# Reordering casts, transposes, loads and one layer's start around a TensorE-bound attention and mixing kernel

## The chip, the cores and the metric

The kernel runs on one core of one Trainium2 chip. The metric is the device time of one execution in microseconds (us). TensorE is the matmul engine (PE in the profile, PEld its weight loads), VectorE is DVE, ScalarE is ACT, GpSimd is POOL, and SP is the sync engine, which here only issues transfers. "Position" below is the start of an instruction in us from the start of the span. PSUM is the memory that the matmuls write into and that the other engines copy results out of.

## The reference, cut to what matters

There are 8 batches. Each goes through cross attention between x (8 heads, 512 rows, 64 wide) and a state of 32 rows, then a two-dimensional Fourier mix, a normalization and a two-layer network (512 to 2048 to 512).

```python
scores  = scale * x @ state.T ;  xread = softmax(scores) @ state      # per head
scores2 = scale * state @ x.T ;  sread = softmax(scores2) @ x
x  = concat([xread, sread]) reshaped to (8, 544, 512)
u  = x + real(fft(fft(x, axis=1), axis=2))
un = (u - mean(u)) / sqrt(var(u) + 1e-6)
out = u + relu(un @ w_ch1) @ w_ch2
```

## The kernel before

Everything is bf16 on TensorE with f32 in PSUM. The program fixes the order of instructions on each engine. From batch 1 on, each period `weave`s several streams by their place between 0 and 1: layer 2 of one batch, layer 1 of the next (`ph`, from `unT`), the reads of attention (`xfp`, `xlp`, `xrp`), the Fourier transform (`gp`, `yp`, then `U`, statistics, `ub`, and its turned form `unT`), the scores (`esp`) of a later one, and loads of x. More names that recur: `warm` are matmuls on the identity whose results nothing uses; `sT` and `xT` are the state and x turned, `eTp` holds scores made from them (or their turned form), `srp` the reads on the state's side; `XF`, `XR`, `XL` are the reads as VectorE copies them out of PSUM, and the fold is the chain, mostly on VectorE, from these to `XQ`, which `gp` needs; `tp` is the turn of `ub` on TensorE; `po` is layer 2's output and `ot` a result tile.

```python
    def cast_x(b):                       # x to bf16
        if b == 0:
            for si in (0, 1, 3):
                nc.scalar.copy(t[:, si, 1:513], xs[:, si, :])
            nc.gpsimd.tensor_copy(t[:, 2, 1:513], xs[:, 2, :])
    ...
    def clears(i):                       # GpSimd, set 0: after it has issued four weight loads
        nc.gpsimd.memset(XFs[i][:, :, 512:514], 0.0)
        nc.gpsimd.memset(XRs[i][:, :, 0:514:513], 0.0)
        ...
        def turn_u(k, r):                # batches 0 and 1: on TensorE, copied out of PSUM
            ...
            if b >= u_by_dma:            # batches 2 and up: by a transposing transfer
                nc.sync.dma_start_transpose(out=unT[:, :, col:col + 128], in_=ub[k, r])
                return
    ...
    for b in range(1, B + 1):
        streams = [(l2_now + ..., 0, 1)]
        if b < B:
            streams.append((layer1(b), 0.08, 1))
        if b + 1 < B:
            streams.append((reads_next, 0, 0.34))
            streams.append((transform(b + 1), 0.47 if b == 1 else 0.4, 0.77 if b == 3 else 0.8))
        ...
        weave(*streams)
```

The softmax here doesn't subtract the row's maximum and nothing guards it: scores larger than these inputs give would overflow.

## Time and profile before

| | before |
|---|---|
| time, median of 4 runs | 315.04 us (314.83 to 316.01) |
| span of the profiled execution | 313.9 us |
| TensorE / VectorE / ScalarE / GpSimd busy | 95% / 59% / 44% / 24% |
| idle TensorE before the first matmul | 3.4 us |
| listed TensorE waits that the change aims at | 3.5 us |

How to read it: the profile's list of waits gives, for each line of TensorE, what ended the idle time before it, the sum, the number and the longest. In a timeline, a row is a start, a duration, the engine, line, operation and tiles, and in brackets the idle time before it with its releaser. The rows themselves are in the prediction.

### The profile page before, as it was taken

Reading aid. Unit: us, or ns where it says so; the run is one execution under the profiler, and the core shown is the slowest. Engines: PE = TensorE matmul, PEld = TensorE weight load, DVE = VectorE, ACT = ScalarE, POOL = GpSimd, SP = SyncE. Lnnn points to the kernel's source line nnn. Section 1 sums busy time; section 2 is a strip of 40 time slices with the busy share of each in tenths; the row PEclk is TensorE's granted clock in tenths of the full one; section 3 lists DMA queues with packets and bytes.
Section 4 is the critical chain, followed back from the end, with each engine's and each line's share of the span. In section 5 each row is a group of like instructions: output and inputs, shape, how many; then the busy total and the mean of one; then the engine's idle time right before and its main releaser. Section 6 shows DMA issues by size and latency. Waiting matters only on the chain.

```text
span 313.9 us, 5948 instructions
## 1 busy us (share of the span) xinstructions
PE 299.2 (95%) x2300; PEld 170.2 (54%) x2300; DVE 185.0 (59%) x442; ACT 137.6 (44%) x268; POOL 75.0 (24%) x171
## 2 busy tenths in 40 slices
PE   5778999999989999999999999999999999999995
PEld 5566997544544555456644554455445544555443
DVE  8696882877767593873817774686559563100012
ACT  6698764735533543243442444333533433333300
POOL 8758784410240040300510024002200131000000
PEclk9999999999999999999999999999999999999999
DMA  9999899965654925349344343631333036303147
GB/s 161 183 200 203 140 177 167 198 123 138 112 101 104 185 68 136 77 102 157 87 84 98 87 102 76 128 83 51 80 75 67 33 84 98 74 34 67 38 100 165
DMA packets 114292, 34.86 MB, mean 111 GB/s; under 512 B 105688, under 2 KB 110040, under 8 KB 114264
## 3 DMA queue, kind: packets, MB, share of 16 engines
q1 hardware_dynamic: 103544, 28.72, 45.8%
q0 software_dynamic: 4224, 4.19, 8.7%
q10 hardware_dynamic: 6496, 1.57, 2.4%
q8 instruction: 18, 0.29, 0.4%
q14 instruction: 10, 0.08, 0.1%
HBM read 22.41 MB, written 14.02 MB: 116 GB/s over the span
## 4 chain that ended last, share of the span: by engine, by line
PE 76%; DVE 15%; DMA 3%; ACT 3%; issue 1%; SPq 0%; DVEq 0%; ACTq 0%
PE po L763 31%; PE ph L698 27%; PE gp L578 3%; PE ph L708 3%; DVE U L548 3%; DVE st L318 2%; DMA xs<-in_x_dram 2%; DVE ub L612 1%; PE po L755 1%; PE xfp L436 1%; PE yp L544 1%; DVE ot L729 1%; PE xrp L436 1%; PE gp L582 1%; PE yp L543 1%
## 5 line engine op out<-in xcount | busy, mean ns | idle before, releaser
L763 PE MATMUL po<-w,hT 128*128 128x512 bf16 x496 | 125.2, 379 | 0.0
L700 ACT ACTIVATE hT<-ph 128x512 bf16<-128x512 f32 x112 | 66.9, 597 | 125.0 <-PE ph L698 125.0
L698 PE MATMUL ph<-unT,w 128*128 128x512 bf16 x448 | 114.6, 379 | 1.4 <-DMA unT<-ub 1.1
L698 PEld LDWEIGHTS <-w 128*128 128x128 bf16 x576 | 51.1, 98 | 49.9 <-issue 2.3
L763 PEld LDWEIGHTS <-hT 128*128 128x128 bf16 x496 | 47.0, 98 | 44.1
L729 DVE SCALAR_TENSOR_TENSOR ot<-po,rstd,U 128x512 f32<-128x512 f32 (+2 forms) x33 | 24.1, 732 | 52.2 <-PE po L763 47.9
L588 POOL COPY GL<-G 128x128 bf16<-128x128 bf16 x8 | 2.3, 292 | 115.7 <-ACT G L586 115.7
L548 DVE TENSOR_TENSOR U<-yp,XR 128x512 f32<-128x512 f32 x16 | 10.9, 682 | 26.4 <-PE yp L544 26.4
L318 DVE BATCH_NORM_STATS2 st<-U 128x6 f32<-128x512 f32 x32 | 21.8, 682 | 0.1
L324 POOL TENSOR_TENSOR rstd<-mv,epst 128x1 f32<-128x1 f32 x34 | 7.1, 210 | 61.8 <-DVE mv L320 61.8
L325 POOL TENSOR_TENSOR rstd<-rstd,mhalf 128x1 f32<-128x1 f32 x34 | 20.9, 614 | 2.7
L586 ACT CAST G<-gp 128x288 bf16<-128x288 f32 x31 | 12.0, 398 | 11.4 <-PE gp L582 6.8
L708 PE MATMUL ph<-unT,w 128*128 128x128 bf16 x256 | 15.9, 219 | 0.7 <-ACT unT L622 0.7
L783 PE MATMUL warm<-ident 128*128 128x128 bf16 x152 | 12.6, 235 | 3.8 <-POOL ident masks.py:199 3.4
L708 PEld LDWEIGHTS <-w 128*128 128x128 bf16 x256 | 15.0, 98 | 0.9 <-issue 0.8
L578 PEld LDWEIGHTS <-XQ 128*128 128x128 bf16 x96 | 8.9, 98 | 8.8 <-DVE XQ L508 2.3
L783 PEld LDWEIGHTS <-ident 128*128 128x128 bf16 x152 | 10.9, 106 | 4.7 <-POOL ident masks.py:199 3.4
L138 POOL CAST xin<-xs 128x2048 bf16<-128x2048 f32 x7 | 13.2, 1889 | 0.1
L612 DVE TENSOR_SCALAR ub<-U,mv 128x512 bf16<-128x512 f32 x24 | 12.3, 511 | 1.1 <-DVE mv L320 0.3
L436 PEld LDWEIGHTS <-ET 128*128 128x128 bf16 x80 | 7.0, 98 | 9.3 <-DVE XF L445 1.6
L445 DVE TENSOR_TENSOR XR<-xrp,rs 128x512 bf16<-128x512 f32 x16 | 11.1, 695 | 1.1 <-POOL XR L278 0.5
L710 ACT ACTIVATE hT<-ph 128x512 bf16<-128x512 f32 x16 | 9.3, 598 | 3.9 <-PE ph L708 3.9
(190 smaller groups left out, 350.5 us busy)
## 6 DMA issues: line engine op xcount, KB each, us to landing
xs<-in_x_dram SPq DMA_DIRECT2D x22, 256.0 KB, 5.3
w<-in_moe_w_ch_dram POOLq DMA_DIRECT2D x8, 512.0 KB, 10.6
out_dram<-ot SPq DMA_DIRECT2D x15, 256.0 KB, 2.5
r_dram<-ot SPq DMA_DIRECT2D x14, 256.0 KB, 2.3
out_dram<-r_dram SPq DMA_DIRECT2D x14, 256.0 KB, 3.8
xs<-in_x_dram SPq DMA_DIRECT2D x8, 192.0 KB, 4.3
xs<-in_x_dram ACTq DMA_DIRECT2D x2, 256.0 KB, 4.9
l_dram<-ot SPq DMA_DIRECT2D x2, 256.0 KB, 2.0
```

Source lines behind the costliest of these rows:

```text
L318: nc.vector.bn_stats(st6, u)
L325: nc.gpsimd.tensor_tensor(rstd, rstd, mhalf, op=ALU.pow)
L436: nc.tensor.matmul(ph[:, 0:260], lhsT=ET[:, g, c0:c0 + 128], rhs=rhs, start=True, stop=True)
L548: nc.vector.tensor_add(u.rearrange("p (k r) -> p k r", r=2), p.rearrange("p (r k) -> p k r", r=2)[:, 0:u.shape[1] // 2, :], x.rearrange("p ...
L578: nc.tensor.matmul(p[:, 0:NM], lhsT=XQ[:, j, c, :], rhs=tab[c], start=(c == 0), stop=(c == 2 and j != 2))
L612: nc.vector.tensor_scalar(t, in0=ud, scalar1=mv[:, 0:1], scalar2=None, op0=ALU.subtract)
L698: nc.tensor.matmul(ph[:, o:o + n], lhsT=w1[:, c, f * 128:(f + 1) * 128], rhs=un_of[key][:, c, :], start=(c == 0), stop=(c == DC - 1))
L700: nc.scalar.activation(hT[:, per * i:per * i + per, :].rearrange("p a b -> p (a b)"), ph, AF.Relu, scale=-1.0 if key in flipped else 1.0)
L708: nc.tensor.matmul(ph[:, o:o + 128], lhsT=w1[:, c, f * 128:(f + 1) * 128], rhs=un_of[key][:, c, 128 * r:128 * r + 128], start=(c == 0), st ...
L729: nc.vector.scalar_tensor_tensor(ot[:, cols], in0=po_of[i][:, 0:cols.stop - cols.start], scalar=rstd, in1=u[:, cols], op0=ALU.mult, op1=AL ...
L763: nc.tensor.matmul(po_of[i], lhsT=h_of[key][:, f, i * 128:(i + 1) * 128], rhs=w2[:, f, :], start=(f == 0), stop=(f == FC - 1))
L783: nc.tensor.matmul(t[:, 0:128], lhsT=ident, rhs=ident, start=(i == 0), stop=(i == n - 1))
```

## The change

The intent: cast and turn batch 0's pieces in the order in which they land, turn the state before x in the sync queue, load x one period later, start the scores of batch 2 and the first layer of batch 2 later, and let layer 1 of batch 0 begin on half a tile.

```diff
-            for si in (0, 1, 3):
+            for si in (0, 3, 1):                      # casts of batch 0
-            for si in (0, 1, 3, 2):
+            for si in (0, 3, 1, 2):                   # turns of batch 0
-                turned[b] = lambda: (turn_x(0), turn_x(1), turn_state())
+                turned[b] = lambda: (turn_state(), turn_x(0), turn_x(1))
+            if (b, k, r) == (0, 0, 1):                # first copy of unT in two halves
+                for j in (0, 2):
+                    nc.scalar.copy(unT[:, j:j + 2, col:col + 128], tp[...])
+                return
-          ..., (scores_next, 0.4, 1), ([lambda: load_x(4)], 0.6, 0.6))
+          ..., (scores_next, 0.46, 1))
-            streams.append((layer1(b), 0.08, 1))
+            streams.append((layer1(b), 0.13 if b == 2 else 0.08, 1))
-        if b + 4 < B:
-            streams.append(([lambda: load_x(b + 4)], 0.35, 0.35))
+        if b + 3 < B:
+            streams.append(([lambda: load_x(b + 3)], 0.35, 0.35))
```

More of the change, by code (lines that the diff above doesn't have):

```diff
@@ L621, in turn_u @@
                 nc.tensor.transpose(tp[:, 128 * j:128 * j + 128], ub[k, r][:, 128 * j:128 * j + 128], ident)
+            if (b, k, r) == (0, 0, 1):
+                for j in (0, 2):
+                    nc.scalar.copy(unT[:, j:j + 2, col:col + 128],
+                                   tp[:, 128 * j:128 * j + 256].rearrange("p (a b) -> p a b", b=128))
+                return
             (nc.vector.tensor_copy if b == 0 and k else nc.scalar.copy)(unT[:, :, col:col + 128], tp[:, 0:512].rearrange("p (a b) -> p a b", b=128))
@@ L805 @@
     weave((L[11:], 0, 0.25), (t1, 0.2, 1), ([M[i] for i in (0, 4, 1, 5, 2, 6, 3, 7, 8, 9)], 0.33, 0.99),
-          ([lambda: state_blocks(3, B, nc.gpsimd.tensor_copy)], 0.35, 0.35), (scores_next, 0.4, 1), ([lambda: load_x(4)], 0.6, 0.6))
+          ([lambda: state_blocks(3, B, nc.gpsimd.tensor_copy)], 0.35, 0.35), (scores_next, 0.46, 1))
     l2 = M
```

## The prediction

> **What bounds the kernel now.** I read the page's busy row first, then its forty slices, then TensorE's list of waits, and last the timelines around those waits.
>
> ```profile
> PE 299.2 (95%) x2300; PEld 170.2 (54%) x2300; DVE 185.0 (59%) x442; ACT 137.6 (44%) x268; POOL 75.0 (24%) x171
> PE   5778999999989999999999999999999999999995
> ```
>
> TensorE is busy for 299.2 of 313.9 us, so all its idle time is 14.7 us, and the second line shows where it lies: in the first four slices of 7.85 us and in the last one, with one dip in slice 12 (about 86 to 94 us). Outside these the kernel can only get faster by doing less matmul work, and the change removes none. In the chain of waits the two layers' matmuls (po L763 and ph L698) hold 31% and 27% of the span. TensorE's waits, over the whole span:
>
> ```profile
> PE warm L783 <- POOL ident masks.py:199: 3.4, 1, 3.4
> PE xTp L375 <- ACT xin L135: 1.4, 2, 1.1
> PE ph L698 <- DMA unT<-ub: 1.1, 1, 1.1
> PE gp L578 <- DVE XQ L508: 0.8, 2, 0.5
> PE ph L708 <- ACT unT L622: 0.7, 1, 0.7
> PE tp L621 <- ACT ub L610: 0.3, 1, 0.3
> ```
>
> The 3.4 us are the wait for the identity at the start, and some 3.6 us more lie after the last matmul (the last result tile is made by VectorE from 310.31 us, then stored). The change touches neither. What is left is 14.7 - 3.4 - 3.6 = 7.7 us. This is a ceiling, and 2% of the time is 6.3 us. Of it the change aims at four lines: L375 (1.4), the DMA of unT (1.1), L622 (0.7) and L610 (0.3), 3.5 us together.
>
> **What the Trainium skill says.** "Perfetto Trace Analysis", Identifying the Most-Contended Engine, warns that matmul busy time is a poor measure of the distance from the roofline. The trace agrees: one 128x512 matmul is recorded as 379 ns, but groups of four start 0.86 us apart, 0.216 us each. So a small gap in issue can hide under the pipelined ends, and I count gaps by start times. The same page, Optimizing Scalar/DVE Operations, says that breaking up an instruction may let work complete sooner where an engine isn't saturated but leaves bubbles on others, and that ScalarE pays a per-instruction overhead of about 51 ns on PSUM. The trace agrees in size: in the chain a 512-wide copy out of PSUM holds ScalarE for 0.49 us and a 1024-wide one for 0.93, so 0.44 per 512 and 0.05 fixed. "DMA: Bandwidth & Descriptors", Anatomy of one DMA, says that a wait on a semaphore is taken by the issuing sequencer and not by the DMA engines. So one waiting transfer holds back what stands behind it in its queue; below, the sync queue shows just that.
>
> **Part 1: casts of batch 0.** Of the four pieces of x, piece 0 lands at 4.84 us, piece 3 (issued by ScalarE at 1.24, 5.7 us to landing) at about 7.0, and piece 1 (sync queue, 1.74 + 6.84) only at 8.58. Before, ScalarE cast 0, then 1, then 3, and stood from 7.5 to 8.6 with piece 3 already there.
>
> ```profile
> 8.60 1.14 ACT L135 CAST xin<-xs 128x512 bf16<-128x512 f32 x2 [1.08 <-DMA xs<-in_x_dram]
> 8.99 0.68 POOL L136 CAST xin<-xs 128x512 bf16<-128x512 f32 x1 [0.32 <-DMA xs<-in_x_dram]
> 9.64 0.58 ACT L364 COPY sT<-sTp 128x512 bf16<-128x512 bf16 x1
> 10.23 1.01 ACT L376 COPY xT<-xTp 128x1024 bf16<-128x1024 bf16 x1
> ```
>
> In the new order cast 3 fits into that hole, cast 1 runs 8.60 to 9.21, and the copy of sT ends near 9.7 in place of 10.22. Taken alone this is 0.53 us. But the turns also need piece 2, which GpSimd finishes at 8.99 + 0.68 = 9.67, whatever ScalarE does. Then come two transposes (0.28 us), so the copy of xT can start near 10.0 and not at 10.23. Worth 0.22 us. Behind it follows a chain of short steps on VectorE, ScalarE and TensorE up to 28 us. I looked in it for fixed points that would swallow the gain: GpSimd's clears (VectorE waits for one at 14.2), ScalarE's sines (to 23.34, then the G copies), GpSimd's cast of batch 1 (ends 25.72, its turns then start at 25.76 in place of 25.84). Each leaves the long VectorE path just enough room. I carry 0.22 us to 28 us.
>
> **Part 2: first unT copy in two halves.** At 28.22 the chain goes through three copies on ScalarE in a row:
>
> ```profile
> 28.22 0.59 ACT unT L622
> 28.81 0.49 ACT sT L389
> 29.30 0.93 ACT xT L390
> ```
>
> The first half of unT is there about 0.22 us sooner, so the first two matmuls of layer 1 start sooner, but the third needs the second half. More important, TensorE waits again at 30.26, for the third of these copies, and that comes one fixed cost, 0.05 us, later. The 0.67 us wait will look shorter, the time gets 0.05 us worse. Parts 1 and 2 together: 0.17 us.
>
> **Part 3: scores of batch 2 later (0.4 to 0.46).** The order of the built program shows the effect: the first eight score matmuls (0.23 us of issue) move behind the first group of second-axis matmuls yp, and the second eight behind one more layer-2 group. All TensorE work is the same. The first yp starts at 53.20 in place of 53.43, and VectorE's run U, statistics, ub, which begins at 54.14 with an idle VectorE, ends 0.23 us sooner. That run sets the 0.29 us wait at 60.35, which falls to about 0.06. Worth 0.23 us.
>
> **Part 4: state of batch 2 ahead of x, and x one period later.** The sync queue waited 6.8 us for GpSimd's cast before it issued xT, with sT behind it:
>
> ```profile
> 39.21 7.11 SPq L369 DMA_TRANSPOSE xT<-xin  x4
> 46.37 4.19 SPq L358 DMA_TRANSPOSE sT<-stb  x2
> 50.61 10.85 SPq L128 DMA_DIRECT2D xs<-in_x_dram  x12
> 61.56 0.35 SPq L744 DMA_DIRECT2D r_dram<-ot  x1
> ```
>
> The blocks of state are ready at 37.2, so sT uses about 2 us of that wait, and the whole group is issued about 2 us sooner. Yet the first scores at 52.33 show no wait in the trace before, so this buys slack and no time. Of the twelve loads, six (x of batch 4) leave this spot, and the first store of a result, ready at 60.16, no longer stands until 61.56. No matmul waits for it. The loads that now follow at 75 us replace equal loads (batch 5 before); batch 7's come into period 4 near 178, where the sync queue has a hole of 3.8 us for about 4.4 us of issue. Its unT is needed some 10 us later. Worth 0.
>
> **Part 5: layer 1 of batch 2 later (0.08 to 0.13).** This is the largest one.
>
> ```profile
> 90.04 1.04 PE L763 MATMUL po<-w,hT 128*128 128x512 bf16 x4
> 92.14 1.02 PE L698 MATMUL ph<-unT,w 128*128 128x512 bf16 x4 [1.06 <-DMA unT<-ub]
> 93.00 0.38 PE L436 MATMUL xfp<-stb,ET 128*128 128x260 bf16 x2
> 93.22 1.03 PE L763 MATMUL po<-w,hT 128*128 128x512 bf16 x4
> ```
>
> unT of batch 2 lands at 92.0. In the new order the pair xfp (0.22 us) and the next group po (0.86) stand ahead of the first ph: 1.08 us of work that needs no unT, against a wait of 1.06. Its inputs are ready: xfp needs the PSUM tile that VectorE frees at 90.18. The wait goes to about 0, worth 1.06 us. Against this, reads and fold of this period come closer together: I place the last read near 96.9, while VectorE, which first makes a result tile (0.75 us) at 95.2, gets to it at 97.7. From there to the first fold output is 3.1 us as before, at 100.8, while TensorE wants it at 100.6. So I take off 0.2 us for a new wait on XQ.
>
> Sum: 0.17 + 0.23 + 0 + 1.06 - 0.2 = 1.26 us. 315.06 - 1.26 = 313.8 us, 0.4% less.
>
> **The rivals.** First, the wait for unT comes back in another place: the VectorE run that makes unT starts from TensorE's own yp at 79.3, so it moves with TensorE and the cover of 1.08 against 1.06 has no margin; a transpose that lands 0.3 us later costs 0.3 us. And the wait on XQ may be 0.5 rather than 0.2. For it: VectorE is busy 9.05 of the 10 us before 90. This makes 314.5. Second, the start gains more than I think: if 0.53 us of the casts count, and the earlier transfers relieve the crowded DMA engines (share near 0.9 from 32 to 64 us), the time is 313.0. Against it: GpSimd's piece ends at 9.67 on its own, and no matmul after 32 us waits for those transfers. Third, the moved loads hurt: batch 7's x ahead of unT of batch 5, or x of batch 4 too late for its cast at 89.05. For it: one queue issues all of it. Against it: x of batch 4 is issued by 80 us and lands within about 6. It would make 315 to 316.
>
> **Range and chances.** The gains that I trust are bounded by the 3.5 us of waits aimed at; the most likely losses undo half of 1.26. With medians that scatter by a few tenths of a us, 312.5 to 314.9 should hold it 8 times in 10. Faster by over 2% needs 6.3 of the 7.7 us that were left in all; slower by over 2% needs a stall far over any wait now on the list.
>
> **What would show it.** Right: the unT wait gone from TensorE's list, the tp wait below 0.1, the ScalarE cast wait shorter and the first eTp near 11.07 instead of 11.29; layer 1 of batch 0 near 28.5, but the second eTp wait still there near 30.1; all TensorE records after 100 us shifted by one constant. Wrong: an XQ wait of half a us or more near 100, an unT wait in any period, TensorE busy time away from 299 us, or a shift at 32 us above 0.4 or below 0.

## The result, and the profile after

| | before | after |
|---|---|---|
| time, median | 315.04 us (4 runs) | 314.04 us (4 runs, 313.97 to 314.52) |
| ratio | | 0.9965, 95% interval 0.9943 to 0.9988 |
| last result tile starts (first trace of each) | 310.31 | 309.12 |

Ratios here and below are the mean time of one kernel's runs over that of the other's in the same rounds, so not quite the ratio of the medians. Executions over 1.5% slower than the fastest of the same kernel are left out of the means. The change gains about 1 us, 0.3%, within the 2% that counts as the same.

The two rows of the page of the changed kernel that answer to those of before, busy time and TensorE's forty slices:

```profile
PE 297.9 (95%) x2268; PEld 171.3 (55%) x2300; DVE 184.9 (59%) x442; ACT 137.7 (44%) x269; POOL 74.8 (24%) x171
PE   5878999999999999999999999999999999999995
```

The dip in slice 12 is gone. The 1.3 us less of busy time is no sign of less work: this trace lacks 32 of the 2300 matmul records, and the change removes no matmul. The list of TensorE's waits over the whole span of the changed kernel:

```profile
PE warm L788 <- POOL ident masks.py:199: 3.4, 1, 3.4
...
PE eTp L400 <- ACT xT L390: 0.5, 1, 0.5
PE ph L713 <- ACT unT L624: 0.5, 1, 0.5
PE xTp L375 <- POOL xin L136: 0.5, 1, 0.5
...
PE tp L621 <- ACT ub L610: 0.3, 1, 0.3
```

The wait for unT's transfer (1.1) has left the list, the first ph waits less for its copy (0.5 after 0.7), and the wait for ScalarE's casts is now one for GpSimd's. But the tp wait is still 0.3. The TensorE timeline of the changed kernel where the long wait was, and where the fold's result is needed:

```profile
90.10 0.81 PE L768 MATMUL po<-w,hT 128*128 128x512 bf16 x3 [0.16 <-issue]
90.75 0.39 PE L436 MATMUL xfp<-stb,ET 128*128 128x260 bf16 x2
90.97 1.03 PE L768 MATMUL po<-w,hT 128*128 128x512 bf16 x4
91.83 1.03 PE L703 MATMUL ph<-unT,w 128*128 128x512 bf16 x4
...
99.40 1.03 PE L768 MATMUL po<-w,hT 128*128 128x512 bf16 x3
100.45 0.42 PE L578 MATMUL gp<-CT,XQ 128*128 128x288 bf16 x2
```

The read xfp and one group of po now stand before ph, and ph follows po in 0.86 us, the pitch of a full group: no gap at all. (The 0.16 us of "issue" at 90.10 is a missing fourth po record.) At 100.45 there is no bracket, yet 99.40 + 0.86 is 100.26: gp starts 0.19 us late, 0.06 us after VectorE's XQ is there (99.83 + 0.56 = 100.39 us). Such a gap nearly vanishes from the record, since a matmul's recorded 379 ns reach 0.16 us past its 0.216 us of issue: po's record ends at 100.43, 0.02 us before gp.

So the place of each shift, after minus before, in the first two traces: the read xlp of batch 0 at 14.97 in both; the first eTp of batch 1 ("the second eTp" for short) at 30.33 after 30.26 (+0.07); the third tp at 60.18 after 60.35 (-0.17); the last tile -1.19. Nothing came from the start, about a quarter of a us from the scores, and the rest from the period of batch 2. After it the shift is one constant: VectorE's first XQ of the later periods, at 135.94, 175.18, 208.02 and 240.87 us before, comes 1.19 to 1.20 us sooner.

### The profile page after: what moved, and what is told of

It is laid out like the page before. It is cut to its first block, busy times and chain, and to the rows that moved or that the text cites. A ratio compares the mean times of both kernels' runs of the same rounds, so it can differ in the third digit from the quotient of the medians.

```text
span 312.3 us, 5918 instructions
## 1 busy us (share of the span) xinstructions
PE 297.9 (95%) x2268; PEld 171.3 (55%) x2300; DVE 184.9 (59%) x442; ACT 137.7 (44%) x269; POOL 74.8 (24%) x171
## 4 chain that ended last, share of the span: by engine, by line
PE 79%; DVE 13%; ACT 2%; DMA 2%; issue 2%; SPq 0%; POOL 0%; DVEq 0%; POOLq 0%; ACTq 0%
PE po L768 32%; PE ph L703 29%; PE gp L578 4%; PE ph L713 3%; DMA xs<-in_x_dram 2%; DVE U L548 2%; DVE st L318 2%; PE po L760 1%; PE yp L544 1%; PE xfp L436 1%; PE xrp L436 1%; PE yp L543 1%; PE gp L582 1%; PE esp L411 1%; DVE XF L445 1%
## 5 line engine op out<-in xcount | busy, mean ns | idle before, releaser
L768 PE MATMUL po<-w,hT 128*128 128x512 bf16 x476 | 122.0, 379 | 1.5 <-issue 0.8
L788 PE MATMUL warm<-ident 128*128 128x128 bf16 x152 | 13.5, 246 | 3.7 <-POOL ident masks.py:199 3.4
L788 PEld LDWEIGHTS <-ident 128*128 128x128 bf16 x152 | 11.8, 113 | 4.7 <-POOL ident masks.py:199 3.4
```

The lines of the kernel that those rows point to most:

```text
L768: nc.tensor.matmul(po_of[i], lhsT=h_of[key][:, f, i * 128:(i + 1) * 128], rhs=w2[:, f, :], start=(f == 0), stop=(f == FC - 1))
L788: nc.tensor.matmul(t[:, 0:128], lhsT=ident, rhs=ident, start=(i == 0), stop=(i == n - 1))
```

## The experiments

Twelve runs were made, ten of new kernels and one more of each of the two, all correct. Runs with five rounds are compared with the kernel before in the same rounds.

**e1: casts alone** (one look).

```diff
-            for si in (0, 1, 3):            # before's casts;   turns: (0, 1, 3, 2)
+            for si in (0, 3, 1):            #                   turns: (0, 3, 1, 2)
```

> Only the new order of casts and turns of batch 0. Theory A (GpSimd's late clear of XR holds VectorE at 14.2 us and so swallows the gain): first eTp near 11.1 us (11.29 before), but xlp at 14.97, the first gp at 21.27 and the first ph of layer 1 at 28.86 as before, and the end at 310.3; time 315.0 within noise. Theory B (the recorded prediction): everything to 28 us is 0.2 us earlier and the last tile is made 0.2 us earlier.

Measured: 314.7 us beside 314.8. First eTp at 11.16, xlp at 15.02, first gp at 21.33, first ph at 28.91, third tp at 60.41. The first eTp is 0.13 us sooner than in the first trace of before, but all that follows, from xlp on, is 0.05 to 0.06 us later: nothing of the start's gain is left. The theory's early part held. But the last tile started at 309.83 and not at 310.3, and not because of the casts: the wait in front of ph in the period of batch 2 was 0.53 us in this trace and not 1.06, in a part of the program that is the same as before. That was the first sign that this wait differs from one execution to the next.

**e2: split copy alone** (one look).

```diff
+            if (b, k, r) == (0, 0, 1):
+                for j in (0, 2):
+                    nc.scalar.copy(unT[:, j:j + 2, col:col + 128], tp[...])
+                return
```

> Only the first unT copy in two halves. Theory A (ScalarE's three copies in a row are the path, so one more fixed cost is paid): first ph at 28.64 in place of 28.86, the first eTp of batch 1 at 30.33 in place of 30.26, and all later TensorE starts 0.06 us later; time 315.1. Rival (the sooner first ph counts): later starts up to 0.2 us earlier.

Measured: 315.11 us beside 314.8. The TensorE timeline of e2:

```profile
28.70 1.22 PE L713 MATMUL ph<-unT,w 128*128 128x128 bf16 x16 [0.46 <-ACT unT L624]
30.38 0.41 PE L400 MATMUL eTp<-xT,sT 128*128 128x288 bf16 x2 [0.47 <-ACT xT L390]
```

Counted from xlp (15.03 here, 14.97 before), ph starts 0.22 us sooner, and eTp and the third tp (60.47) 0.06 us later. ph takes 1.22 us and not 1.05, since it waits inside for the second half. The split trades a shorter wait for a longer one behind it and loses 0.06 us. Theory A stands.

**e3: scores alone** (one look).

```diff
-          ..., (scores_next, 0.4, 1), ([lambda: load_x(4)], 0.6, 0.6))
+          ..., (scores_next, 0.46, 1), ([lambda: load_x(4)], 0.6, 0.6))
```

> Only the scores of batch 2 later (0.46). Theory A (the VectorE run that begins with the first yp sets the pace from 54 to 60 us): first yp at 53.20 (53.43 before), third tp at 60.12 (60.35 before), last tile 0.23 us earlier (310.08), with the wait of 0.29 still listed because TensorE's hidden gaps before it shrink instead. Rival (the prediction's form): the same 0.23 us, but the listed wait falls to 0.06. Second rival: the score matmuls were what mattered and nothing moves (60.35).

Measured: 315.41 us beside 314.8, with a wait for unT of 1.15 us in this trace. The TensorE timeline before, and that of e3:

```profile
58.48 0.26 PE L423 MATMUL eTp<-mirror,E 128*128 128x96 bf16 x2
58.81 0.38 PE L621 MATMUL tp<-ident,ub 128*128 128x128 bf16 x4
...
60.35 0.40 PE L621 MATMUL tp<-ident,ub 128*128 128x128 bf16 x4 [0.29 <-ACT ub L610]
```

```profile
58.41 0.26 PE L423 MATMUL eTp<-mirror,E 128*128 128x96 bf16 x2
58.63 0.38 PE L621 MATMUL tp<-ident,ub 128*128 128x128 bf16 x4
...
60.18 0.34 PE L621 MATMUL tp<-ident,ub 128*128 128x128 bf16 x3 [0.30 <-ACT ub L610]
```

From xlp, the third tp is 0.23 us sooner (60.18 - 15.03 against 60.35 - 14.97). The step from 58.48 to 58.81 was 0.33 us and is 0.22. In the same way the first tp stood 0.13 us behind the end of issue of the po group before it (56.26 + 0.86 to 57.25) and now stands none (57.18). These two gaps between starts, which no list shows, are the gain; the listed wait is the same. My expectation had also put the last tile at 310.08; it came at 310.24, since the wait for unT was longer in this trace.

In this one trace the 0.23 us did not reach the end. Counted from xlp, the last tile stands at 295.21 us, and in e12, which has no edit, at 295.23: unT landed no sooner (ph stands 77.03 us behind xlp, 77.05 in e12), so the wait in front of ph took the gain back. With layer 1 later it comes through: from xlp, the last tile of the changed kernel stands at 294.15 in both its traces, and that of e7, which lacks the edits to casts, split, scores and state, at 294.33. The difference of 0.18 us is about 0.23 for the scores less 0.06 for the split (e2).

**e4: state first alone** (one look).

```diff
-                turned[b] = lambda: (turn_x(0), turn_x(1), turn_state())
+                turned[b] = lambda: (turn_state(), turn_x(0), turn_x(1))
```

> Only the state turned ahead of x, in every batch from 2. Theory A (slack only): sync queue done with the six transposes of batch 2 near 48.6 us in place of 50.56, no TensorE start moves by more than 0.05 us before 85 us; the third transpose of unT (86.92) may be issued in a shorter time because the loads ahead of it go 2 us earlier, and then the wait of 1.06 at 92 us shrinks by up to 0.7. Rival: all transfers are hidden and 1.06 stays.

Measured: 315.9 us beside 314.8. In this execution the first x came late (second cast at 8.99, first eTp at 11.76, xlp at 15.41), so all of it is 0.4 us late. From xlp, the third tp (60.79) is at 45.38 as before. The sync queue was done with the six transposes at 49.6 us in place of 50.56 (48.6 expected). The wait for unT was 0.95. No gain is seen; the hoped-for effect on unT isn't either.

**e5: x one period later alone** (five rounds).

```diff
-          ..., ([lambda: load_x(4)], 0.6, 0.6))
-        if b + 4 < B: ... load_x(b + 4)
+        if b + 3 < B: ... load_x(b + 3)
```

> Only x one period later. Theory A (the last unT transpose stood behind a third one whose issue took 2.48 us because of transfers in flight; with x's loads earlier out of the queue it takes 1.9 and unT lands near 91.2 and not 92.0): the wait of ph on unT falls from 1.06 to about 0.3, and the last tile is made about 0.7 us earlier; ratio 0.998. Rival (recorded prediction: hidden, worth 0): wait stays 1.06 and the time is that of before.

Measured: 314.96 us beside 315.01; ratio 0.9998 (0.9985 to 1.001). The wait was 0.53 us in its trace, shorter as theory A wanted (about 0.3), but e1 shows 0.53 with the loads in their old place, and the time shows no gain. Theory A is not borne out; the prediction's zero stands within the interval, which leaves room for 0.5 us of gain.

**e6: layer 1 of batch 2 later alone** (five rounds), and **e7: this and e5's edit** (five rounds).

```diff
-            streams.append((layer1(b), 0.08, 1))
+            streams.append((layer1(b), 0.13 if b == 2 else 0.08, 1))
```

> Only layer 1 of batch 2 later. Counted by starts the gap before is 1.24 us (90.90 to 92.14), the cover 1.08. Theory A (unT still lands at 92.0 without the moved loads): a gap of 0.16 us stays in front of ph, and some 0.2 us is lost at XQ near 100; last tile 0.9 us earlier (309.4), ratio 0.997. Rival (the layer's place is all of the gain): no gap at ph, last tile 1.06 us earlier.

> x one period later and layer 1 of batch 2 later together. Theory A: gap at ph gone (1.24 us), XQ gap of 0.19 us near 100; last tile 1.05 us earlier (309.26), ratio 0.9965, nearly all of the whole change's 1.19. The two alone overlap: less than the sum of e5 and e6. Rival (they add): 1.6 us or more.

Measured: e6 314.57 us beside 315.01, ratio 0.9982 (0.9969 to 0.9995); e7 314.4 us, ratio 0.9979 (0.9968 to 0.9991). The TensorE timeline of e6:

```profile
91.29 1.03 PE L763 MATMUL po<-w,hT 128*128 128x512 bf16 x4
92.15 1.03 PE L698 MATMUL ph<-unT,w 128*128 128x512 bf16 x4
```

ph follows po at the full pitch, so there is no gap even without the moved loads: the rival is right on this and my 0.16 us of residue is not there. From xlp, the last tiles come 1.03 us (e6: 309.44, xlp 15.13) and 1.01 us (e7: 309.31, xlp 14.98) sooner than in the first trace of before. The gap by starts was 92.14 - 90.90 = 1.24 us; less the 0.18 us that e7 loses at XQ (99.58 + 0.86 to 100.62), this is 1.06. So x later adds nothing to the layer's new place. The timed gains are smaller than the traces' 1.0: 0.2% is about 0.6 us. A likely reason, not tested by itself, is that the kernel before usually waits less than in its first trace (see e12).

**e8: the changed kernel with XF's and XR's clears moved to VectorE's start** (five rounds), and **e10: the same edit on the kernel before** (one look).

```diff
     def clears(i):
-        nc.gpsimd.memset(XFs[i][:, :, 512:514], 0.0)
-        nc.gpsimd.memset(XRs[i][:, :, 0:514:513], 0.0)
+        if i == 1:
+            nc.gpsimd.memset(...)   # both, as before
+    nc.vector.memset(XFs[0][:, :, 512:514], 0.0)         # early, at allocation
+    nc.vector.memset(XRs[0][:, :, 0:514:513], 0.0)
```

> The changed kernel, and the clears of XF and XR of set 0 made by VectorE at the start and not by GpSimd behind its weight loads. Theory A (that clear is what swallowed the casts' gain): VectorE's first XR starts near 13.3 us in place of 14.22, xlp near 14.2 in place of 14.97, and 0.4 to 0.7 us arrive at the first ph of layer 1 (28.64), unless ScalarE's sines or GpSimd's cast of batch 1 hold it; last tile near 308.6 against 309.12; ratio to before 0.995. Rival (another fixed point, such as GpSimd's fold behind its weight loads, holds the chain anyway): first ph within 0.1 us of 28.64.

> The kernel before with the clears of set 0 on VectorE at the start. Theory A (the clear and the cast order hold xlp to nearly the same moment, so neither alone helps): xlp within 0.05 us of 14.97 counted from the same start, first ph at 28.85 within 0.05. Rival (the clear alone was the hold, cast order irrelevant): xlp near 14.8, first ph near 28.7.

Measured: e8 314.14 us beside 315.01, ratio 0.997 (0.9956 to 0.9983); first ph at 28.49 (28.64 in the changed kernel), last tile at 308.95 (309.12). e10 314.91 us beside 315.4; first ph at 28.66. The VectorE timeline of before in its second trace (e12), and that of e10:

```profile
14.21 0.69 DVE L445 TENSOR_TENSOR XR<-xrp,rs 128x512 bf16<-128x512 f32 x1 [0.69 <-POOL XR L278]
```

```profile
13.57 0.70 DVE L448 TENSOR_TENSOR XR<-xrp,rs 128x512 bf16<-128x512 f32 x1
```

GpSimd's clear in e12, and the TensorE timeline of e12 and of e10:

```profile
14.01 0.17 POOL L278 MEMSET XR<- 128x4 bf16 x1
```

```profile
14.96 0.40 PE L436 MATMUL xlp<-stb,ET 128*128 128x260 bf16 x2
```

```profile
14.77 0.39 PE L439 MATMUL xlp<-stb,ET 128*128 128x260 bf16 x2
```

Without the clear, VectorE turns the first read into XR 0.64 us sooner, frees its PSUM tile, and xlp starts at 14.77 (e10) or 14.82 (e8), not at 14.96 to 14.97, and the 0.15 to 0.2 us arrives at the first ph. I had hoped for 0.4 to 0.7 us: the next hold is TensorE's own group srp, behind which xlp stands in its queue: without the clear (e8, e9, e10) xlp follows the first eTp by 3.65 to 3.66 us, and so it does in e4, where x came too late for the clear to matter. My theory for e10, that the clear alone wouldn't help, fell for this execution; its rival is right. Where x lands early, the clear is what held the start under either order of casts. Where it lands as late as in the first trace of before, 11.29 + 3.65 is 14.94 us, so there the clear alone would be worth only about 0.03 us by this estimate. By time, e8 is not shown to be faster than the changed kernel: its ratio is that of e11.

**e9: e8 with the first unT copy whole again, and e11: the changed kernel again** (five rounds, same rounds).

```diff
-            if (b, k, r) == (0, 0, 1):     # the split of unT's first copy, taken out of e8
-                ...
```

> The changed kernel with the clears of set 0 on VectorE at the start and unT's first copy whole again. Theory A: the gain of the clears (0.15 us, seen) and that of the whole copy (0.06 us) add: first eTp of batch 1 near 30.11, last tile near 308.9; 0.2 us faster than the changed kernel of the same rounds, too little to be clear in the medians. Rival (the split's sooner first ph was worth something): last tile not before 308.95.

> The changed kernel again, in the same rounds as e9. Both theories: ratio to before 0.9965 to 0.998, as the wait for unT in the kernel before differs between executions (0.5 to 1.2 us in the traces that keep layer 1 in its old place); last tile near 309.1.

Measured: e9 314.07 us, ratio to before 0.9957 (0.9944 to 0.9971); e11 314.46 us, ratio 0.997 (0.9957 to 0.9984). From xlp (14.91), e9's second eTp is at 15.29, as in before, so the 0.06 us is back. Its last tile starts at 308.98, although batch 0's x came later in this execution (first eTp at 11.26 against 11.13 in e11). e9 has the lowest ratio and the lower median of its rounds, but the intervals overlap, so I don't call it shown to be faster than the changed kernel. e8's last tile, 308.95, is not bettered as it stands; counted from xlp, e9's comes 0.06 us sooner (294.07 against 294.13), the size of the split's loss.

**e12: the kernel before, a second trace** (one look).

```diff
 (no edit)
```

> The kernel before, unchanged, in a second trace. Theory A (piece 1's landing and the unT transposes differ between executions of one program, and the first trace had both late): second cast of batch 0 starts between 8.0 and 8.5 us (8.60 in the first trace), first eTp between 11.08 and 11.2 (11.29), xlp still near 14.97 to 15.1; the wait for unT between 0.5 and 1.2 us. Rival (the first trace is what this program does, and the moved parts of the other kernels changed these): 8.60, 11.29 and 1.06 again within 0.03.

Measured: 315.21 us beside 315.04. The ScalarE timeline, then the TensorE timeline of e12:

```profile
7.91 1.14 ACT L135 CAST xin<-xs 128x512 bf16<-128x512 f32 x2 [0.64 <-DMA xs<-in_x_dram]
8.96 0.58 ACT L364 COPY sT<-sTp 128x512 bf16<-128x512 bf16 x1
10.04 1.01 ACT L376 COPY xT<-xTp 128x1024 bf16<-128x1024 bf16 x1 [0.50 <-PE xTp L375]
```

```profile
92.01 1.02 PE L698 MATMUL ph<-unT,w 128*128 128x512 bf16 x4 [0.94 <-DMA unT<-ub]
```

Theory A holds but for the second cast, which came at 7.91, below my range. With the old order of casts, xT's copy stood 0.50 us waiting for the turns, which wait for GpSimd's piece 2 (8.75 + 0.91 = 9.66). ScalarE had finished the casts and sT by 9.54. First eTp is at 11.10, the same as the changed kernel's 11.11. The first trace of before, on which the prediction rests, had caught piece 1 late.

The wait for unT, in the eight traces that keep layer 1 in its old place, is 1.06 (before), 0.94 (e12), 0.53, 0.92, 1.15, 0.95, 0.53 (e1 to e5) and 0.61 (e10), on average 6.69 / 8 = 0.84 us. In e1 and e5 the profile names a VectorE step, L482, that ended at about the same time; I take it for the same wait. Why unT lands early in some executions stays open: the third of its four transposes took 2.48 us to issue in before and 1.19 in e1, but also 1.19 in e3, which waited longest (there the last transpose took 3.4 us from issue to landing). So the issue time of the third alone does not explain it, and no experiment controlled it.

## Why the prediction was right or wrong

The time (313.8 against 314.04 measured) and the class were right, and the largest step was the one that it named. Several of the small steps were not.

- **What bounds it**: right. The whole gain came out of TensorE's waits or gaps; after the change TensorE is still busy 95% of the span. The ceiling of 7.7 us counts recorded idle time only, and gaps by starts are longer, as below.
- **Part 1, casts, 0.22 us**: wrong; it arrives as 0. Two things failed. The step "Each leaves the long VectorE path just enough room" is wrong for the first of the fixed points that it lists: GpSimd's clear holds VectorE's XR to 14.2 us, and xlp can't start before XR has emptied the PSUM tile, at 14.97 in both kernels. In the trace that the prediction read, VectorE already stood idle for 0.51 us in front of this clear, so the path had no room to gain there. Moving the clear in e10 and e8 shows it. And the 10.23 of xT's copy was a late execution, not the rule: e12 has 10.04 with the old order. When x comes late, as in e4, the new order might still help; that wasn't tried.
- **Part 2, split, a loss of 0.05 us**: right in sign and mechanism, measured as 0.06 (e2), and e9 takes it back.
- **Part 3, scores, 0.23 us**: right in size (e3), wrong in how it would show in the profile. The wait at 60.35 did not fall "to about 0.06"; it stayed at 0.30, and the gain lay in smaller gaps between starts just before it. It also depends on part 5: alone, in e3's one trace, it was lost again in front of ph.
- **Part 4, state and loads, 0**: right. e5 gives a ratio of 0.9998 (its interval allows a gain of 0.5 us or a loss of 0.3); e4, one look, shows no earlier position.
- **Part 5, layer 1 later, 1.06 less 0.2**: the mechanism is right and both terms are seen, the wait gone and 0.19 us lost at XQ. Its net worth of 0.86 us came out nearly right by luck, since two errors cancel. The prediction took the recorded wait, 1.06, although it meant to count by starts; by starts the gap was 1.24 us in that trace. But the wait is usually shorter than in that trace: over eight traces the listed wait is on average 0.84, about 1.0 by starts with the hidden 0.17. So the usual worth is about 1.0 - 0.19 = 0.8 us, and the timed 0.2% of e6 and e7 (0.6 us) agrees within its interval.
- **The rivals**: the first did not come: XQ cost 0.19 us, as the prediction itself had it, and not 0.5, and ph follows without a gap in all six traces with layer 1 later. Its point that the cover has no margin holds, though: in e3 the gap by starts was 1.3 us (92.06 against 90.75), more than the cover of 1.08. The second and third did not come. By the prediction's own test, "a shift at 32 us above 0.4 or below 0" was to show it wrong, and the shift there is about 0.06 us to the late side: that test rightly pointed at part 1. Of its signs of being right, the unT wait that is gone, the first eTp (11.11), the second eTp wait that stays and the constant shift came; the tp wait below 0.1 did not, and layer 1 of batch 0 began at 28.64, not near 28.5.
- **The sum**: 0 - 0.06 + 0.23 + 0 + 0.8 = about 1.0 us, estimated from the terms above, against the 1.0 us between the medians and 1.26 predicted. The difference of some 0.27 us is nearly all part 1's 0.22.

## What to carry to other kernels

Follow a gain to the first fixed point behind it, above all to the PSUM tile that the next matmul needs and to whoever holds its emptying; the casts' gain died at a clear of four columns that stood behind weight loads. Do not add gains as if each stood alone: the scores' 0.23 us reached the end only once the wait behind it was covered. On a bound TensorE, count gaps between starts, not brackets, and cover a late transfer by moving matmuls that don't need it in front of it. Take a second trace of the unchanged kernel before sizing any wait that ends in a transfer.

## What the Trainium skill lacked or had wrong

- "Perfetto Trace Analysis", Identifying the Most-Contended Engine, rightly distrusts matmul busy time. It doesn't say that idle time between matmul records is too small as well: here by 0.16 to 0.18 us for each gap behind 128x512 matmuls (1.24 us by starts where the record shows 1.06, and 0.19 us where the list of waits shows none).
- The same page, Optimizing Scalar/DVE Operations, says that breaking up instructions may help where an engine that isn't saturated causes bubbles. It doesn't say when it won't: here ScalarE was busy 44% of the span and the split still cost time, because three of its copies in a row were the path: 0.06 us lost, close to the overhead of about 51 ns that the page gives for PSUM.
- No page that I read gives how far landing varies between executions of the same program: the second cast of batch 0 started at 7.91 us in one trace of the kernel before and at 8.60 in the other. The wait for the transposed tile was 0.94 and 1.06 us in these two, and from 0.53 to 1.15 over the eight traces, which are of seven kernels.
